# Two small products between TensorE's load of the verdict and its branch

## The chip, the cores and the metric

The kernel runs on one core of a Trainium2 chip. A core has TensorE (PE, the matmul array, with weight loads shown as PEld), VectorE (DVE), ScalarE (ACT), GpSimd (POOL) and SyncE (SP, which here issues the stores). Each engine has its own instruction stream, with a sequencer (shown with a q: DVEq, PEldq) that waits for semaphores, takes branches and hands instructions to the engine. Sixteen DMA engines serve all the queues. The metric is the device time of one execution in microseconds; the profile is of one more execution, whose time stands in the table below. Fp32 throughout.

## The reference

```python
# gated linear attention, B=4, H=8, S=768, D=48
state = alpha[:, :, t, :, None] * state + einsum('bhd,bhe->bhde', k[:, :, t], v[:, :, t])
y[:, :, t] = einsum('bhd,bhde->bhe', q[:, :, t], state)
# x: (B, H, S, D) -> (3072 tokens, 384)
h = x @ w_in          # 384 x 2048
g = h - tanh(h)
out = g @ w_out       # 2048 x 384
```

## The kernel before

The 3072 tokens are worked through in twelve units of 256. Of each unit the attention is computed first, and then its block with tanh in eight steps of 256 columns of the hidden layer: first products into h, h - tanh(h) as a polynomial on ScalarE and VectorE, second products into the output sums. From the seventh unit on the first products, and from the third on the second products, are made with fewer block products on combinations of blocks (Strassen's manner). So a unit's result does not lie in PSUM as such: it lies in four sums o0 to o3, which store() turns into two tiles. ScalarE scales o2 into p52, then VectorE makes four sums with put(), each 128 x 384: same = o1 + p52, cross = o1 - p52, same = same + o3, same = same + o0. Then SP issues four stores, two of cross and two of same.

The polynomial holds for small h alone, and the weights are rounded in a way that holds for a range alone. So the kernel gathers evidence while it works (tiles over, sizes, least, most, tiny). judge() (L1454 on) reduces it to one column, gather() (L1469) transposes that column with a matmul into one row of a PSUM tile of two banks (two_banks), VectorE reduces the row to one word ok (L1475), and see() (L1477) loads ok into a register of every engine. Behind fast() stands a branch (L1522): where ok is 0, every engine runs general(), a slow way that always holds; where it is 1, as here, every engine jumps over it to the closing semaphores. The code of general() lies between the branch and its target. On TensorE that is some 800 instructions.

The order of all work is written out. A planner lists tasks with an engine, a cost, a rank and what they come after, a long list of steps gives their order, and the instructions are emitted in that order, each into its engine's stream. The last tasks are the second products of the last step, see, and store of the last unit, which is emitted after see: so on each engine the load of the verdict stands ahead of what store() emits there, and behind store() comes the branch. TensorE has no instruction of store(): its last products of o3 and o0 come ahead of its load, and its branch follows the load at once. Semaphores are added by the framework wherever an instruction reads what another engine wrote or overwrites what another engine reads.

Lines that matter below: L1358 second products; L1418 p52 on ScalarE; L1421 the four sums in put() on VectorE; L1429 the stores; L1471 the transpose and L1475 the reduction of the verdict; L1478 its load; L1522 branch and what stands at its target; L1549 the closing barrier.

Of the kernel before, what the change touches and what calls it, by code (L numbers as in the profile page):

```python
# [17 lines left out]
HP = 64  # L18
# [415 lines left out]
def fast(tc, q, k, v, alpha, moe_w_in, moe_w_out, out, w_in, w_out, ident, ok, pad_rows):  # L434
# [7 lines left out]
    NU = B * UPB  # L442
# [7 lines left out]
    V, A, T, GP = nc.vector, nc.scalar, nc.tensor, nc.gpsimd  # L450
# [3 lines left out]
    with ExitStack() as ctx:  # L454
# [90 lines left out]
        def two_banks():  # L545
            return ps_sc.tile([P, 2, NP, P], FP32, name="sc")
# [30 lines left out]
        for n, (what, s) in enumerate(pieces):  # L577
            rank = RANK[what] + 2 * s
            held = pieces[n - 4] if n >= 4 else None
            both = what == "in" and s < BOTH_QUEUES  # L580
# [656 lines left out]
        def moe(u, rank, gait):  # L1237
# [170 lines left out]
            def store():  # L1408
                o = m["o"]
                if plain:  # L1410
                    for c in range(CU):
                        ob = two.tile([P, d_model], FP32, name=("same", "cross")[c], bufs=1)
                        A.mul(ob, o[c], 1 / W_SCALE)
                        nc.sync.dma_start(out=out_r[u * CU + c], in_=ob)
                    return

                p52, same, cross = (two.tile([P, 2, NH], FP32, name=n, bufs=1) for n in ("p52", "same", "cross"))
                A.mul(p52, o[2], 1 / W_SCALE)  # L1418

                def put(out, of, op, more):  # L1420
                    V.scalar_tensor_tensor(out=out, in0=of, scalar=1 / W_SCALE, in1=more, op0=ALU.mult, op1=op)  # L1421
                put(same, o[1], ALU.add, p52)
                put(cross, o[1][:, ::-1, :], ALU.subtract, p52)
                put(same, o[3], ALU.add, same)
                put(same, o[0][:, 0:1, :].to_broadcast([P, 2, NH]), ALU.add, same)
                for t, to in ((cross, 1), (same, 0)):
                    for c in range(CU):
                        n = abs(to - c)
                        nc.sync.dma_start(out=out_r[u * CU + c][:, n * NH:(n + 1) * NH], in_=t[:, c, :])  # L1429
            add(f"store {u}", "DVE", 2.1 if not plain else 0.1, rank + gait * FS + 4.9,  # L1430
                [f"second {u}:{FS - 1}", u == NU - 1 and "see"], store, lat=1.0)
            yield

# [18 lines left out]
        verdict = {}  # L1452
# [14 lines left out]
            verdict["fine"] = fine  # L1467

        def gather():  # L1469
            verdict["row"] = two_banks()[:, 0, 0, :]  # L1470
            T.transpose(verdict["row"][0:1, :], verdict["fine"][:, 0:1], ident)  # L1471
        add("judge", "DVE", 1.2, 16 * NU, [f"large {last_step}", f"x {NU - 1}.{CU - 1}", f"least {NU - 1}"] + [f"look {n}" for n in range(len(pieces))], judge)
        add("gather", "PE", 0.3, 16 * NU - 20, ["judge"], gather)
        add("ok", "DVE", 0.3, 16 * NU, ["gather"],
            lambda: V.tensor_reduce(out=ok, in_=verdict["row"][0:1, :], axis=AX.X, op=ALU.min))  # L1475
# [78 lines left out]
```

## Time and profile before

| | |
|---|---|
| median of 3 runs | 558.7 us (557.97, 558.70, 559.77) |
| profiled execution, its own time | 559.94 us |
| its span, first to last instruction | 558.12 us |
| busy: PE, DVE, ACT, POOL | 547.1, 462.2, 357.3, 4.9 us |
| granted TensorE clock | 0.999 |
| code loads: q8 (TensorE's), q14 (the others') | 49 of 16 KB, 24 of 8 KB |
| stores from L1429, issue to landing | 1.6 to 3.9 us, median 1.7 |

The page gives the busy time of each engine and its share of the span. Below the page the trace can be asked for a line, a stretch or a queue: times in such answers are from the start of the span, an arrow in brackets names what ended the idle time ahead of an instruction, and the number ahead of it is that idle time. Code loads are the DMA of instructions into an engine's instruction memory. The landing of a store is reported in 16 parts, one for each DMA engine. Where a time is given with three decimals or as a packet's start or end, it is read from the trace's records of instructions, DMA packets and semaphores.

### The profile page before, as it was taken

To read this page: it belongs to the slowest core of one execution; us is meant where nothing else is said; L and a number is where in the kernel's file an instruction comes from. 1 tells how busy PE (TensorE), PEld (TensorE's weight loads), DVE (VectorE), ACT (ScalarE), POOL (GpSimd) and SP (SyncE) were. 2 spreads that over 40 slices of the span, in tenths; PEclk is the share of its full clock that TensorE was granted. 3 is DMA by queue.
4 is the path that set the end of the run, shared out by engine and by line. 5 is a ranking of instruction groups with operands and counts; after the bars stand their busy time and mean duration, and the time that the engine had idled before them with its cause. 6 is when DMAs were issued, how large, how long until landed. Compare 5 with 4: busy or idle time off the path is not lost. (4 is left out here: it accounts for less than half of the span.)

```text
span 558.1 us, 14664 instructions
## 1 busy us (share of the span) xinstructions
PE 547.1 (98%) x6045; PEld 497.3 (89%) x6045; DVE 462.2 (83%) x853; ACT 357.3 (64%) x722; POOL 4.9 (1%) x23
## 2 busy tenths in 40 slices
PE   8999999999999999999999999999999999999995
PEld 7787777779998999999999999899999999999995
DVE  7988799999998597598896799999899856765764
ACT  3699995648666677667794556768556544545550
POOL 3000000000000000000000000000000000000000
PEclk9999999999999999999999999999999999999999
DMA  9999862144682483464540041311200000000001
GB/s 237 199 249 259 283 144 58 30 119 117 131 161 69 93 207 98 113 128 137 156 136 0 31 94 30 80 43 31 56 10 3 29 8 3 31 7 1 29 2 33
DMA packets 60233, 50.86 MB, mean 91 GB/s; under 512 B 35552, under 2 KB 49920, under 8 KB 60160
## 3 DMA queue, kind: packets, MB, share of 16 engines
q1 hardware_dynamic: 57536, 49.07, 35.1%
q8 instruction: 49, 0.80, 0.6%
q10 hardware_dynamic: 2624, 0.79, 0.6%
q14 instruction: 24, 0.20, 0.1%
HBM read 44.04 MB, written 4.72 MB: 87 GB/s over the span
## 5 line engine op out<-in xcount | busy, mean ns | idle before, releaser
L1256 PE MATMUL h<-xT,w_in 128*128 128x256 f32 (+1 forms) x588 | 131.2, 377 | 1.4 <-DVE w_in L92 0.7
L1256 PEld LDWEIGHTS h<-xT,w_in 128*128 128x128 f32 x588 | 108.7, 190 | 16.8 <-DVE w_in L92 1.1
L1358 PE MATMUL o<-b,e 128*128 128x192 f32 x480 | 93.3, 327 | 0.0
L1358 PEld LDWEIGHTS o<-b,e 128*128 128x128 f32 x480 | 78.9, 191 | 0.4
L1358 PE MATMUL o<-w_out,e 128*128 128x192 f32 x320 | 78.7, 328 | 0.4 <-issue 0.4
L1312 DVE SCALAR_TENSOR_TENSOR g<-z,w 128x512 f32<-128x512 f32 x96 | 64.7, 683 | 5.5 <-ACT z L1303 2.3
L1358 PE MATMUL o<-b,g 128*128 128x192 f32 x320 | 68.8, 326 | 0.0
L1303 ACT ACTIVATE z<-u 128x512 f32<-128x512 f32 x96 | 60.4, 632 | 3.7 <-DVE g L1312 2.1
L1293 DVE TENSOR_TENSOR w<-h,u 128x512 f32<-128x512 f32 x48 | 33.0, 686 | 34.5 <-PE h L1288 34.5
L1299 ACT ACTIVATE u<-w 128x512 f32<-128x512 f32 x48 | 30.0, 627 | 41.9 <-DVE w L1293 41.7
L1358 PEld LDWEIGHTS o<-w_out,e 128*128 128x128 f32 x320 | 55.1, 191 | 1.7 <-issue 0.5
L1267 PE MATMUL h<-xT,w_in 128*128 128x128 f32 x288 | 54.7, 278 | 0.2
L1280 ACT COPY u<-h 128x128 f32<-128x128 f32 x96 | 24.6, 265 | 47.1 <-PE h L1267 47.0
L1358 PEld LDWEIGHTS o<-b,g 128*128 128x128 f32 x320 | 53.8, 191 | 0.1
L1267 PE MATMUL h<-xT,w_out 128*128 128x128 f32 x288 | 53.3, 275 | 0.0
L1318 ACT ACTIVATE big<-u 128x1024 f32<-128x1024 f32 x48 | 50.7, 1056 | 0.6
L1267 PEld LDWEIGHTS h<-xT,w_in 128*128 128x128 f32 x288 | 48.2, 191 | 2.4 <-ACT xT L1038 0.4
L1288 PE MATMUL h<-xT,w_in 128*128 128x256 f32 x192 | 48.9, 380 | 0.0
L1299 ACT ACTIVATE u<-h 128x512 f32<-128x512 f32 x48 | 28.5, 594 | 29.5 <-PE h L1256 29.3
L1325 DVE TENSOR_TENSOR e<-g 128x384 f32<-128x384 f32 x80 | 44.1, 551 | 2.6 <-PE o L1358 0.8
L1308 DVE TENSOR_TENSOR w<-h,u 128x512 f32<-128x512 f32 x48 | 32.6, 682 | 15.5 <-ACT u L1299 15.5
L1267 PEld LDWEIGHTS h<-xT,w_out 128*128 128x128 f32 x288 | 44.1, 192 | 0.1
(171 smaller groups left out, 969.8 us busy)
## 6 DMA issues: line engine op xcount, KB each, us to landing
raw<-in_moe_w_out_dram SPq DMA_DIRECT2D x16, 768.0 KB, 6.1
raw<-in_moe_w_in_dram SPq DMA_DIRECT2D x48, 96.0 KB, 5.3
raw<-in_moe_w_in_dram SPq DMA_DIRECT2D x16, 288.0 KB, 5.3
vt<-in_v_dram SPq DMA_DIRECT2D x23, 192.0 KB, 3.7
ar<-in_alpha_dram SPq DMA_DIRECT2D x20, 192.0 KB, 3.3
kr<-in_k_dram SPq DMA_DIRECT2D x20, 192.0 KB, 3.2
qr<-in_q_dram SPq DMA_DIRECT2D x20, 192.0 KB, 3.2
raw<-in_moe_w_in_dram SPq DMA_DIRECT2D x16, 192.0 KB, 5.4
```

Source lines behind the costliest of these rows:

```text
L1256: T.matmul(h[:, a, to], lhsT=w_in[:, j, f * P:(f + 1) * P], rhs=xT[u][:, j, to], start=(j == 0), stop=(j == KT - 1))
L1267: T.matmul(m["h", s][:, to], lhsT=left[n][:, s], rhs=right[u][n], start=start, stop=True, skip_group_check=True)
L1280: A.copy(m["kept", s][:, n], m["h", s][:, 3])
L1288: T.matmul(m["h", s][:, 2 * a:2 * a + 2].rearrange("p i t -> p (i t)"), lhsT=wi[:, KT - 1, s, a], rhs=xT[u][:, KT - 1, :], start=False, st ...
L1293: V.tensor_add(m["w", s], m["h", s].rearrange("p i t -> p (i t)"), m["u", s])
L1299: A.activation(m["u", s], m["h", s], AF.Square, scale=W_SCALE ** -1.5)
L1303: A.activation(m["z", s], m["u", s], AF.Square, bias=QB, scale=QA * W_SCALE)
L1308: V.tensor_mul(m["w", s], m["h", s], m["u", s])
L1312: V.scalar_tensor_tensor(out=g.rearrange("p a c t -> p (a c t)"), in0=m["z", s], scalar=QK, in1=m["w", s], op0=ALU.add, op1=ALU.mult)
L1318: A.activation(big, m["us", s // 2].rearrange("p s t -> p (s t)"), AF.Relu, bias=-U_FAST, scale=W_SCALE, accum_out=over[:, n:n + 1])
L1325: V.tensor_sub(e[:, 0:3, :], x[:, 3:4].to_broadcast([P, 3, P]), x[:, 0:3])
L1358: T.matmul(o[n][:, i], lhsT=g_, rhs=w_, start=(s_ == 0 and (n, i) in ((0, 0), (1, 0), (2, 1), (3, 0))), stop=(s_ == FS - 1), skip_group_ch ...
```

## The change

When store() handles the last unit, two matmuls are emitted behind the first sum. Each multiplies the identity with the first 64 columns of same, and writes 64 columns of the second bank of the PSUM tile whose first bank held the verdict's row. Nobody reads them. For this gather() keeps the whole tile as verdict["both"]. In TensorE's stream they come behind the load of the verdict and ahead of the branch.

```diff
                 put(same, o[1], ALU.add, p52)
+                if u == NU - 1:
+                    for n in range(2):
+                        T.matmul(verdict["both"][:, 1, n, 0:HP], lhsT=ident, rhs=same[:, 0, 0:HP], start=True, stop=True)
                 put(cross, o[1][:, ::-1, :], ALU.subtract, p52)
                 put(same, o[3], ALU.add, same)
                 put(same, o[0][:, 0:1, :].to_broadcast([P, 2, NH]), ALU.add, same)
...
         def gather():
-            verdict["row"] = two_banks()[:, 0, 0, :]
+            verdict["both"] = two_banks()
+            verdict["row"] = verdict["both"][:, 0, 0, :]
             T.transpose(verdict["row"][0:1, :], verdict["fine"][:, 0:1], ident)
```

P is 128, HP is 64, NH is 192, NU is 12 and u is the unit. The orders of the other engines' instructions stay as they were.

## The prediction

> **What bounds the kernel now.** The page comes first.
>
> ```profile
> span 558.1 us, 14664 instructions
> PE 547.1 (98%) x6045; PEld 497.3 (89%) x6045; DVE 462.2 (83%) x853; ACT 357.3 (64%) x722; POOL 4.9 (1%) x23
> ```
>
> TensorE bounds the body, but nothing in the body is touched: the change lies in the last 9 us. So the second view is the timeline from 549 us (start, length, engine, line, operation).
>
> ```profile
> 549.54 2.11 PE L1358 MATMUL o<-b,e 128*128 128x192 f32 x12
> 549.74 0.49 ACT L1418 ACTIVATE p<-o 128x384 f32<-128x384 f32 x1 [5.11 <-PE o L1358]
> 550.26 0.56 DVE L1421 SCALAR_TENSOR_TENSOR same<-o,p 128x384 f32<-128x384 f32 x1 [1.55 <-ACTq L1522]
> 550.74 0.55 DVE L1421 SCALAR_TENSOR_TENSOR cross<-o,p 128x384 f32<-128x384 f32 x1
> 551.20 1.21 DVE L1421 SCALAR_TENSOR_TENSOR same<-o,same 128x384 f32<-128x384 f32 x2
> 551.31 0.81 SPq L1429 DMA_DIRECT2D out_dram<-cross  x2
> 552.44 0.82 SPq L1429 DMA_DIRECT2D out_dram<-same  x2
> ```
>
> Four sums, four stores; the last store is issued at 552.81 and yet the span lasts to 558.12. The third view is the line of the branch, which every engine runs after its load of the verdict (PEldq is TensorE's sequencer; shortest, median and longest in ns, first and last start).
>
> ```profile
> L1522 POOLq COMPARE_BRANCH  x1: 45/45/45, 549.3 to 549.3; - x1
> L1522 PEldq COMPARE_BRANCH  x1: 3762/3762/3762, 549.4 to 549.4; - x1
> L1522 ACTq COMPARE_BRANCH  x1: 50/50/50, 549.7 to 549.7; - x1
> L1522 DVEq COMPARE_BRANCH  x1: 72/72/72, 551.9 to 551.9; - x1
> L1522 PEldq EVENT_SEMAPHORE  x1: 51/51/51, 553.2 to 553.2; - x1
> L1522 SPq COMPARE_BRANCH  x1: 50/50/50, 553.3 to 553.3; - x1
> ```
>
> TensorE's branch takes 3.76 us. The DMA records say why: q8, which TensorE's code comes over, moves 16 KB from 550.40 for 1.38 us; TensorE goes on at 553.12 and 0.84 us later q8 moves another 16 KB. That one is in the fourth view, the DMA queues from 553.95 to 555.56 (packets, MB, share of 16 engines).
>
> ```profile
> q1 hardware_dynamic: 76, 0.05, 9.5%
> q8 instruction: 1, 0.02, 6.2%
> ```
>
> The fifth are the landings of the two last stores of `same`, and what SP waits for at the end (us in all, times, longest).
>
> ```profile
> DMA to landing us min/median/max: 2.2/3.0/3.8
> ```
>
> ```profile
> SPq L1522 <- SPq L1522: 3.0, 3, 2.0
> ```
>
> The last store lands 3.8 us after its issue, the one before it after 2.2. Of its 16 parts 15 have landed by 554.93, most by 554.52; the sixteenth at 556.61. Its eight packets start at 555.53, when the fetch (553.96 for 1.59 us) ends: one DMA engine served the code first. SP waits 2.0 us for it and then needs 1.5 us of closing semaphores. So the end is set by the last landing, and that by TensorE's second code fetch: 556.61 - 554.93 = 1.68 us.
>
> **The change, part by part.** It adds two fp32 products on TensorE, eight instructions (weight load and matmul, two passes each), in the stretch between its load and its branch; no other engine gets an instruction or another order, no DMA is added. But each product reads `same` and the third sum overwrites it. Two waits follow: TensorE's first added load waits for the first sum, with the branch alone behind it; VectorE's third sum waits for the second product, with the fourth sum, the two stores of `same` and VectorE's branch behind it.
>
> *The branch.* The first sum ends at 550.82. TensorE reaches the added load at about 549.36, where the branch stood, and waits 1.5 us. Does the sequencer wait, or only the array? On ScalarE the branch starts 6 ns after an ACTIVATE that had waited 5.11 us, on VectorE 24 ns after the fourth sum: the wait holds the sequencer. With 0.03 us to wake and eight issues (bounds 0.02 us each, a semaphore instruction of 17 to 21 ns, and 0.08, the array's own pace) the branch starts at 551.05 to 551.5; I take 551.1, since 30 instructions stood issued ahead in this very stretch. By the row's own offsets the first fetch runs 552.1 to 553.5, TensorE goes on at 554.9 and the second fetch runs 555.7 to 557.3.
>
> *The third sum.* The array is busy until the last product of o0, whose last pass starts at 551.33. The added passes queue behind: the first 0.16 us later (the pitch of 192 columns), three more at 0.11 us (two passes of 128 columns take 0.38 with 278 ns each, so 0.105 apart; 64 columns are no slower), 551.81, and 0.23 to 0.28 to the end: 552.04 to 552.09. VectorE followed TensorE by 0.02 at the verdict's reduction, so the third sum starts at 552.09 instead of 551.20: +0.89. Its 0.56 is unchanged, and the fourth follows 0.03 to 0.09 behind as now. The stores of `same` go out 0.82 to 0.89 later; I take 0.85: 553.29 and 553.66.
>
> *The last landing.* Undisturbed parts land 1.71 us after issue (554.52), disturbed by other engines' fetches 2.12 (554.93): 555.37 to 555.78, and I take 555.5, as the 8 KB fetch of 553.06 that held up the 554.93 part is by then over. Against 556.61 that is -1.1 us (-0.8 to -1.25). TensorE's first fetch now falls on the stores of `cross`, which have until 555 to land: nothing, unless it lasts 1 us longer. TensorE itself is through at 555.0; SP needs that at 556.2. If that cover goes, the closing barrier waits for TensorE instead.
>
> Sum for the profiled execution: span 558.12 - 1.1 = 557.0, and with the 1.82 us around it (559.94 - 558.12) 558.84.
>
> *Against the median.* The profiled execution lies 1.24 above the median of 558.7 and 0.17 above the highest run; the runs spread 1.80, close to the 1.68 that the late part costs. The race is near: that engine's eight packets were due from 553.77 and need 0.26 us, the fetch came at 553.96. I read the lowest run (557.97) as one that escaped. For it the change is a loss: 554.93 (or 554.52) becomes 555.5, +0.6 to +0.9, hence 558.6 to 558.8; the highest becomes 559.77 - 1.1 = 558.7. Both ends meet, so the changed kernel should show 558.6, hardly off the median, with less spread.
>
> *A rule against the rows.* The Trainium skill, "Runtime: NRT & Kernel Launch", section "Instruction fetch mechanics", says that a taken branch out of the two-page window stalls for the target page, and that crossing a 16 KiB boundary is mostly hidden. The stall agrees with 3.76 us here. By the second half the fetch at 553.96 would cost nothing and the change would be a pure loss of 0.85; the row prices that fetch at 1.68, and the row decides.
>
> **The rivals.**
>
> (A) Slower: the second fetch again meets the last store. The engine that carries q8 is free at 553.5 and must then pass 16 packets of `cross` and 16 of `same` before 555.7: 69 ns each. For: after the 16 KB fetch the eight packets took 85 to 98 ns. Against: after the 8 KB fetch of 552.80 they went at 33 ns at once. If it happens, the last part starts at 557.3, takes 0.6 and lands 0.46 later, 558.4: +1.8 on the profiled run, 560.4 to 561.6 in the timed ones.
>
> (B) Faster by over 0.3%: the third sum hardly waits and the collision goes. The last landing is then 554.5 to 554.9, -1.7 to -2.1: 556.6 to 557.0 from the median. Against it stands the array's queue, worked out above. With the delay, and if all three runs had been hit alike, it is 558.7 - 1.1 = 557.6, inside the bound.
>
> (C) The change doesn't move the branch, because the wait sits in the array's queue. The fetches stay, the stores come 0.85 later into the fetch of 553.96, and 16 packets instead of eight wait for 555.55: landing 556.9 to 557.3, +0.3 to +0.7, 559.0 to 559.4. The ScalarE row speaks against it.
>
> (D) TensorE ends last: if the closing code needs the second page, it waits for 557.3 and the 1.3 us that lay between fetch and resumption, 558.6, where the closing steps of 557.55 are now due at 556.4: +1.1, 559.8. Against: TensorE's closing rows are few.
>
> **How the numbers follow.** 0.3%, 1.68 us, is about what a measurement of this kernel can tell from no change. Forecast 0.56, C 0.09 and D 0.05 lie within it; A 0.18 is slower; B 0.10 is faster, and 0.01 is left to either side for what I don't see. So faster 0.11, same 0.70, slower 0.19. The time is the forecast's, 558.6. The range leaves out the worse half of A and nearly all of B: from 557.3 (all runs hit, largest gain 1.25, with 0.15 for the spread) to 560.5 (A's near end).
>
> **What would show it.** TensorE's branch at 551.1 and still some 3.8 us long; third sum at 552.1; stores of `same` at 553.3 and 553.7; the second 16 KB after 555.5; the last landing under 2.2 us from issue; span 557.0. Wrong if the branch stays at 549.4 (C), if the last landing is again over 3.5 us (A), or if the third sum starts before 551.8 (B).

## The result, and the profile after

The changed kernel takes 561.1 us, the median of six runs (560.5 to 562.92); the kernel before took 558.64 in the six runs beside it (557.97 to 559.77). The ratio is 1.0034 with a 95% interval of 1.002 to 1.0048: slower by 1.9 us (1.1 to 2.7); the two medians lie 2.5 us apart, inside that interval. The forecast was 558.6 with 560.5 as its upper end. The profiled execution took 560.74 us, its span is 559.0, and the 1.7 us around the span are close to the 1.8 of before.

The page first: the totals, which show that the body is as it was, with the four added matmuls in PE's count.

```profile
span 559.0 us, 14671 instructions
PE 547.3 (98%) x6049; PEld 497.5 (89%) x6049; DVE 462.5 (83%) x853; ACT 357.3 (64%) x722; POOL 4.9 (1%) x23
```

Then the timeline of the changed kernel at its end (start, length, engine, line, operation).

```profile
549.77 0.56 DVE L1421 SCALAR_TENSOR_TENSOR same<-o,p 128x384 f32<-128x384 f32 x1 [1.54 <-ACTq L1526]
550.24 0.55 DVE L1421 SCALAR_TENSOR_TENSOR cross<-o,p 128x384 f32<-128x384 f32 x1
550.82 2.53 SPq L1432 DMA_DIRECT2D out_dram<-cross  x2
550.84 0.58 PEld L1425 LDWEIGHTS sc<-same,ident 128*128 128x128 f32 x4
551.00 0.55 PE L1425 MATMUL sc<-same,ident 128*128 128x64 f32 x4
551.59 1.15 DVE L1421 SCALAR_TENSOR_TENSOR same<-o,same 128x384 f32<-128x384 f32 x2 [0.80 <-PE sc L1425]
553.45 0.97 SPq L1432 DMA_DIRECT2D out_dram<-same  x2
```

The products and the third sum behave as forecast: the sum waits 0.80 us for the second product. The surprise is in SP's row: the two stores of `cross` took 2.53 us to issue, where the kernel before needed 0.81. The rows of the stores, first that of `cross` before and then those of the changed kernel (shortest, median and longest in ns, first and last start; below them issue to landing) show that it was the second of the pair, with 2156 ns instead of 431.

```profile
L1429 SPq DMA_DIRECT2D out_dram<-cross x2: 332/382/431, 551.3 to 551.7; - x2
```

```profile
L1432 SPq DMA_DIRECT2D out_dram<-cross x2: 332/1244/2156, 550.8 to 551.2; - x2
L1432 SPq DMA_DIRECT2D out_dram<-same x2: 430/462/494, 553.5 to 554.0; - x2
...
DMA to landing us min/median/max: 1.8/3.3/3.6
```

The rows of the branch, and of the closing barrier, of the changed kernel (PEldq is TensorE's sequencer; a DRAIN is the instruction with which an engine reports to the closing barrier), and last TensorE's DRAIN in the kernel before:

```profile
L1526 PEldq COMPARE_BRANCH  x1: 3898/3898/3898, 550.4 to 550.4; - x1
...
L1526 DVEq COMPARE_BRANCH  x1: 72/72/72, 552.2 to 552.2; - x1
L1526 PEldq EVENT_SEMAPHORE  x1: 51/51/51, 554.3 to 554.3; - x1
```

```profile
L1553 SPq DRAIN  x3: 7/7/7, 558.2 to 558.5; - x3
...
L1553 PEldq DRAIN  x2: 8/8/8, 557.7 to 558.6; - x2
```

```profile
L1549 PEldq DRAIN  x2: 8/8/8, 553.3 to 557.7; - x2
```

TensorE's first DRAIN stands at 557.7, 3.4 us behind its first closing semaphore at 554.3; before, it stood at 553.3, 0.15 behind the semaphore. It is late now, but SP's, which waits for the last store, is later still: 558.2. SP's longest wait there is 2.2 us:

```profile
SPq L1526 <- SPq L1526: 2.7, 2, 2.2
```

The body up to the tail differs from execution to execution (the first of the four sums starts anywhere from 549.2 to 550.5 us in the fourteen traces of this case), so from here on all times of the tail are counted from the start of the first sum, and "tail" is what lies from there to the end of the span. They are read from the records of instructions, DMA packets and landings. "First load" and "second load" are the two 16 KB code loads of q8.

| us behind the first sum's start | before | after | difference |
|---|---|---|---|
| TensorE's branch | -0.906 | 0.617 | +1.52 |
| first load, start and end | 0.138, 1.517 | 1.636, 3.211 | +1.50, +1.69 |
| third and fourth sum start | 0.939, 1.590 | 1.818, 2.410 | +0.88, +0.82 |
| length of the issue of the second `cross` store | 0.431 | 2.156 | +1.73 |
| `same` stores issued | 2.175, 2.551 | 3.684, 4.223 | +1.51, +1.67 |
| second load, start and end | 3.695, 5.286 | 5.380, 6.659 | +1.69, +1.37 |
| last landing | 6.344 | 7.733 | +1.39 |
| TensorE's first closing DRAIN | 3.064 | 7.938 | +4.87 |
| tail | 7.860 | 9.249 | +1.39 |

The loss is in the last landing, to the hundredth, and that follows the end of the second load in both kernels, 1.06 us and 1.07 us behind it. Of the changed kernel's last store fifteen of sixteen parts had landed by 5.92; the sixteenth came at 7.73, after that load.

### The profile page after: what moved, and what is told of

It reads as the page before. It is cut to its first block, busy times and chain, and to the rows that moved or that the text cites. A ratio compares the mean times of both kernels' runs of the same rounds, so it can differ in the third digit from the quotient of the medians.

```text
span 559.0 us, 14671 instructions
## 1 busy us (share of the span) xinstructions
PE 547.3 (98%) x6049; PEld 497.5 (89%) x6049; DVE 462.5 (83%) x853; ACT 357.3 (64%) x722; POOL 4.9 (1%) x23
## 4 chain that ended last, share of the span: by engine, by line
PE 93%; DVE 3%; ACT 2%; issue 1%; POOL 0%; DVEq 0%; ACTq 0%; POOLq 0%
PE o L1358 32%; PE h L1256 22%; PE h L1267 13%; PE o L1336 7%; PE h L1288 7%; PE h L989 4%; PE sc L962 1%; PE sc L1135 1%; DVE same L1421 1%; PE sc L969 1%; PE sc L989 1%; PE turned L731 1%; DVE w L1293 1%; ACT u L1299 1%; PE spin L1443 0%
```

## The experiments

Three explanations stand against each other, told here by name. **The issue stall**: SP's second `cross` store is held up by the first load, which now runs while it is issued; the `same` stores go out late and meet the second load again. **The sums' delay**: the third sum's 0.88 us alone make the difference. **The late DRAIN**: the eight added TensorE instructions shift the closing code within its pages (the 16 KB pieces that a load brings), so that TensorE's DRAIN waits for the second load. In the recorded expectations theory 1 is the forecast's own account (the waits and a race), the late DRAIN is theory 3, and the sums' delay is theory 2 (in the first of them that number means something else). The stall has no place in the first four; it first stands as the rival in the last of the second four, and then as theory 6. The medians of the kernel before were 559.29, 559.65 and 559.18 us beside the first, second and third four kernels; a kernel is compared only with the median beside it.

### The first four: what each part does alone

*The kernel before once more*, no edit.

> The kernel before, unchanged, to see its spans run by run. Theory 1 (a race between TensorE's second code load and the last store): the time is about 558.6, and the profile shows one of two pictures: the last store landing 3.8 us after its issue with a time near 559.9, or within 2.2 us with a time near 558. Theory 2 (the late landing belongs to every execution, the spread of the runs comes from the body): the last store lands 3.5 us or more after issue also in an execution of 558.6 or less.

It took 559.48 us, ratio 1.0006 (0.9984 to 1.0028). The row of issue to landing of its stores, and below it that of the next kernel, have the late part again:

```profile
DMA to landing us min/median/max: 1.6/2.0/3.8
```

```profile
DMA to landing us min/median/max: 1.6/2.0/3.9
```

The collision with the second load is in each of the three profiled executions that have stores and code loads at the times of before. That speaks for a regular collision, and not for a race that some executions escape; that some of the timed executions, which have no trace, escape it isn't excluded.

*The products without their read of `same`*: same instructions in the same places, but no wait in either direction.

```diff
-T.matmul(verdict["both"][:, 1, n, 0:HP], lhsT=ident, rhs=same[:, 0, 0:HP], start=True, stop=True)
+T.matmul(verdict["both"][:, 1, n, 0:HP], lhsT=ident, rhs=ident[:, 0:HP], start=True, stop=True)
```

> The two products stay where the change puts them, but read the identity instead of the first sum: TensorE waits for nothing, VectorE waits for nothing, eight instructions more in TensorE's code. Theory 1 (the waits do it): branch of TensorE at 0.9 us ahead of the first sum as before, third sum undelayed, time as before, 558.3 to 559.0. Theory 3 (the code moved by eight instructions so that TensorE's closing DRAIN lies in the next code page): the DRAIN comes 1.3 us behind the end of the second 16 KB load instead of 0.15 us behind the branch, and the time is 0.5 to 1.5 above before, 559.1 to 560.1.

It took 558.99 us, ratio 1.0 (0.9977 to 1.0022); its tail is 7.927. Branch, loads, sums and stores stand where they stood before. One thing has moved, in these rows of the branch and of the closing barrier:

```profile
L1526 PEldq EVENT_SEMAPHORE  x1: 51/51/51, 552.2 to 552.2; - x1
```

```profile
L1553 PEldq DRAIN  x2: 8/8/8, 555.9 to 556.7; - x2
```

The first DRAIN comes 3.7 us behind the semaphore instead of 0.15, and 1.37 behind the end of the second load. So the late DRAIN is the work of the eight instructions, not of the read. Here it is hidden: SP is ready 0.43 later (7.131 against 6.704). Eight more instructions on TensorE, with no wait, cost nothing that the interval (some 1.2 us to either side) can tell.

*VectorE's wait without TensorE's*: on the kernel before, two sums that nobody reads, behind the `cross` sum.

```diff
                 put(cross, o[1][:, ::-1, :], ALU.subtract, p52)
+                if u == NU - 1:
+                    idle = two.tile([P, N * (P + 1)], FP32, name="idle", tag="junk", bufs=1)[:, 0:d_model]
+                    for n in range(2):
+                        V.tensor_add(idle, same.rearrange("p a n -> p (a n)"), p52.rearrange("p a n -> p (a n)"))
```

> The kernel before with two idle sums of 128x384 on VectorE ahead of the third sum, which holds it up by about 0.93 us as the change does (0.88), while TensorE's code and its branch stay. Theory 1: the second code load (4.6 us behind the unmoved branch) now catches both stores of the last tile in every execution; last landing 0.3 to 0.7 later than in the disturbed execution of before, time 560.0 to 560.6. Theory 2 (VectorE's wait is all the cost, at its length): 558.64 + 0.93 = 559.6. Theory 4 (the moved branch is what costs): 559.2 to 559.6, and clearly under the 561.1 of the change.

It took 559.48 us, ratio 0.9999 (0.9977 to 1.0021), although the third sum came 1.24 us late, more than the 0.88 of the change. The 1.4 to 2.0 us of theory 1 lie outside that interval; the 0.9 of theory 2 does not, so the times alone don't exclude it. In the trace it isn't there: the tail is 7.714, below 7.860. The second load ran at 3.315 to 4.566, before most of the late stores, and the last landing at 6.198 no longer followed it: all sixteen parts of the last store landed from 6.02 on. What made them late is in this row:

```profile
L1433 SPq DMA_DIRECT2D out_dram<-same x2: 332/727/1122, 553.3 to 553.6; - x2
```

A store issued in the time of a code load is held up here too: the second store of `same` took 1.122 us, and was through 0.363 us after the second load's end. The delayed sums thus traded one loss for another of about its size.

*The change with two filler products left out at the start of the program*, so that TensorE's closing code lies at the same offset as before (`spin` emits products that only fill TensorE's time; nobody uses their results).

```diff
+        left_out = []
+
         def spin(by=ident):
+            left_out.append(by)
+            if len(left_out) in (10, 11):
+                return
...
```

> The change with two filler products (eight instructions) of TensorE's start left out, so that all code from there on lies in its pages as before. Theory 3: TensorE's closing DRAIN comes within 0.2 us of the branch's end, and if the DRAIN of 557.7 had a part in the end, the time falls by 0.5 or more, to 560.6 or less. Theory 1: the DRAIN moves, the time doesn't: 560.7 to 561.3, since the last landing stands at 557.5 in either case.

It took 558.66 us, ratio 0.9993 (0.9973 to 1.0014), not to be told from before. TensorE's DRAIN came at once (4.204, behind a branch that ended at 3.996). But in the profiled execution a second thing was gone, which this edit doesn't touch:

```profile
L1432 SPq DMA_DIRECT2D out_dram<-cross x2: 332/382/431, 550.8 to 551.1; - x2
L1432 SPq DMA_DIRECT2D out_dram<-same x2: 332/382/431, 552.7 to 553.1; - x2
...
DMA to landing us min/median/max: 1.9/2.3/2.7
```

No store was held up. The first load started where it does in the changed kernel (1.636) and was short, 0.966 us instead of 1.575. The `same` stores went out at 2.995 and 3.371 (+0.82 to before, the sums' delay), the last landing was at 5.239, the tail 6.756: 1.10 us below before. Two explanations now shared the loss, and one kernel that misses both didn't tell them apart.

### The second four: which of the two

*The change once more*, no edit.

> The change, unchanged, beside the next three on one chip. Theory 3 (the eight instructions put TensorE's closing DRAIN on the next code page, and the closing barrier then waits for that page): 1.0 to 2.5 us over before, and the DRAIN at the end of the second 16 KB load + 1.3 us, 7.3 to 8.0 us behind the start of the first sum. Theory 5 (it was that chip or that hour): as the realigned kernel, about before.

560.74 us, ratio 1.0021 (1.0004 to 1.0038), 1.1 us over the median beside it. Issue of the second `cross` store 2.315 us, last landing 8.144 (1.08 behind the second load), DRAIN 8.514 (7.3 to 8.0 had been expected), tail 9.660. Both are there again.

*The realigned change once more*, the same kernel as above.

> The change with two filler products of TensorE's start left out, a second time. Theory 3: 1.5 to 2.5 us below the change itself, 0.3 to 1.1 below before; DRAIN within 0.2 us of the branch's end, last landing 5.2 to 5.6 behind the start of the first sum. Theory 5: equal to the change within 0.5.

560.94 us, ratio 1.0026 (0.9997 to 1.0055), where 1.5 to 2.5 us below the change had been expected of the late DRAIN. Two of its eleven runs lay at 558.4 to 558.7, the others at 560.2 or more, where eight of twelve had been at 558.07 to 558.80 the first time. The rows of the profiled execution, its stores and then its closing barrier:

```profile
L1432 SPq DMA_DIRECT2D out_dram<-cross x2: 332/1274/2217, 550.9 to 551.3; - x2
...
DMA to landing us min/median/max: 1.8/3.5/3.8
```

```profile
L1558 PEldq DRAIN  x2: 8/8/8, 554.8 to 559.1; - x2
```

The DRAIN comes at 554.8, at once, and the tail is still 9.633. The late DRAIN falls as the cause of the loss in this execution: the stall is enough by itself. The first load lasted 1.634 us here; the second ended at 7.060, and nine packets of the last store started only from 7.045 on, where all others had started by 5.62. The landing was at 8.117. The same program thus either stalls or doesn't.

*One product instead of two.*

```diff
-                    for n in range(2):
+                    for n in range(1):
```

> The change with one product instead of two: four instructions instead of eight, no filler left out. The closing EVENT_SEMAPHORE of the changed kernel (two instructions ahead of the DRAIN) still came at once, so the page ends at most two instructions behind it; with four instructions less the DRAIN lies ahead of the end. Theory 3: DRAIN at once again, third sum 0.22 earlier than in the change, time as the realigned kernel or 0.2 better. Theory 1 (the wait and the race alone): as the change, less 0.2.

560.5 us, ratio 1.0019 (0.9998 to 1.0041), tail 9.264. The third sum came at 1.595 instead of 1.818, the issue still took 2.038 us, and ended 0.370 after the first load:

```profile
L1432 SPq DMA_DIRECT2D out_dram<-cross x2: 332/1185/2038, 551.0 to 551.4; - x2
```

```profile
L1553 PEldq DRAIN  x2: 8/8/8, 558.1 to 558.8; - x2
```

The time decides nothing: with 560.94, 560.74 and 560.5 us the realigned change, the change and this kernel lie too close in these four to tell either theory from the other. In the trace the stall sets the stores' time, not the sums. The DRAIN was a miss: it was expected at once with four added instructions and is late (8.147, 1.47 behind the second load). Where the closing code crosses into the second page was counted wrongly; why four suffice stays open.

*The products read `cross` instead of `same`*, behind the `cross` sum, realigned as above: the third sum is free of the wait, the branch waits 0.46 us longer still.

```diff
                 put(cross, o[1][:, ::-1, :], ALU.subtract, p52)
+                if u == NU - 1:
+                    for n in range(2):
+                        T.matmul(verdict["both"][:, 1, n, 0:HP], lhsT=ident, rhs=cross[:, 0, 0:HP], start=True, stop=True)
                 put(same, o[3], ALU.add, same)
```

> The realigned kernel with the products reading cross, which nobody overwrites: VectorE's third sum has no TensorE product to wait for (-0.88), the branch comes 0.47 later than in the change (1.1 behind the start of the first sum). Theory 1: first code load at 2.1 to 3.5, stores of same issued at 2.2 and 2.6 as before, second code load from 5.5, behind the last landing of 4.4 to 4.9; end 0.4 to 0.9 below the realigned kernel. Rival: the first code load now holds up one DMA engine while SP issues, the issue of the next store stalls by 0.7 to 1.7 as in the change, and nothing is gained on the realigned kernel.

559.12 us, ratio 1.0 (0.9978 to 1.0022), 0.5 below the median beside it without being told from it. Branch at 1.080, first load from 2.138 to 3.858. The `cross` stores were out by then, and the stall moved to the next pair that is issued in the time of the load:

```profile
L1432 SPq DMA_DIRECT2D out_dram<-same x2: 332/977/1622, 552.1 to 552.4; - x2
```

It ended 0.316 after the load. The last store landed at 5.687, ahead of the second load (6.026), and the tail is 7.203. The stall is what the expectation's rival forecast, and the landing misses the 4.4 to 4.9 of its theory 1. So a stall costs little where what it delays still passes ahead of the second load.

### The third four: the stores on two queues

If an issue is held up because two stores stand in one queue behind a load, the second store of each pair on ScalarE's idle queue should not be. The edit, alone and on three of the kernels above:

```diff
-nc.sync.dma_start(out=out_r[u * CU + c][:, n * NH:(n + 1) * NH], in_=t[:, c, :])
+(nc.scalar if u == NU - 1 and c else nc.sync).dma_start(out=out_r[u * CU + c][:, n * NH:(n + 1) * NH], in_=t[:, c, :])
```

*On the kernel before.*

> The kernel before, with the second of the two stores of cross and of the two of same of the last unit issued by ScalarE, which is idle by then. Nothing else is changed. Theory 6 (the end is the last landing, late by TensorE's second code load; a queue has one store outstanding on the engine that loads code, a second one stalls): both stores of same are issued 2.18 behind the start of the first sum, their packets are through by 3.5, ahead of the second load at 3.7; last landing 4.1 to 4.6 instead of 6.3 to 6.4, tail from the first sum 5.8 to 6.4 instead of 7.9, time 1.5 to 2.1 below before. Rival: ScalarE's own branch and code load move to 3.6 and catch the stores, landing 5 or later, gain under 1.

558.19 us, ratio 0.9985 (0.9973 to 0.9996): the lowest median of all, 1.0 us below that of the kernel before beside it. That is less than the 1.5 to 2.1 us expected. The timeline and the landings:

```profile
550.85 0.33 SPq L1429 DMA_DIRECT2D out_dram<-cross  x1
550.86 0.37 ACTq L1429 DMA_DIRECT2D out_dram<-cross  x1
551.98 0.33 SPq L1429 DMA_DIRECT2D out_dram<-same  x1
551.98 0.37 ACTq L1429 DMA_DIRECT2D out_dram<-same  x1
```

```profile
DMA to landing us min/median/max: 1.7/2.1/2.5
```

The last store goes out 0.37 earlier than before, and none of its packets waits for the end of the second load (3.677 to 4.841): all had started by 4.003. Last landing 4.639 instead of 6.344, tail 6.229 instead of 7.860. The collision that the kernel before pays in its trace is worth these 1.63 us of tail; the 0.6 us between that and the medians' difference were not traced.

*On the change, realigned.*

> The change with the two filler products left out and the stores on two queues. The sums stay 0.82 late and the branch stays moved. Theory 6: no issue waits for the first code load any more (0.3 to 0.5 instead of 2.0 to 2.3 us), both stores of same go out at 3.0, land by 5.3, ahead of the second load at 5.4; tail 6.6 to 6.9 instead of 9.2 to 9.7. Theory 2 (the sums' delay is the cost): issue times don't matter, the tail stays 8.5 or more.

558.77 us, ratio 0.9988 (0.9979 to 0.9997). No stall (issues of 0.33 and 0.37 us, the last pair at 2.996), the DRAIN at 4.920, last landing 5.568, tail 7.159. The sums' delay is there in full and the kernel isn't slower than before, so this delay alone doesn't make the change slower. It isn't free either, now that the collision is gone: against *two_queues* the tail is 0.93 longer and the median 0.6 higher, though the intervals don't separate the two. The tail is a little above the 6.6 to 6.9 expected; now the load came late: it started at 2.165, 1.55 after the branch, where it otherwise took 1.0.

*On the change as it is.*

> The same without the fillers left out: TensorE's closing DRAIN comes late again, 1.3 to 1.5 us behind the end of the second code load. If that DRAIN can set the end where the stores don't, the tail is 8.5 to 9.2, about 2 us over the realigned one; if the closing barrier doesn't depend on it, 6.6 to 6.9 as there.

560.62 us, ratio 1.0027 (1.001 to 1.0043). Here no store is late (last landing 5.462), and it is as slow as the change. The rows of the closing barrier and SP's wait:

```profile
L1553 SPq DRAIN  x3: 7/7/7, 556.5 to 558.0; - x3
...
L1553 PEldq DRAIN  x2: 8/8/8, 557.7 to 558.0; - x2
```

```profile
SPq L1553 <- PEq L1553: 1.8, 2, 1.3
```

SP is ready at 556.5 and waits 1.3 us for TensorE, whose DRAIN comes at 557.7, 1.284 behind the second load; the tail is 8.219, under the 8.5 to 9.2 expected. Against the realigned kernel with the same queues the tail is 1.06 longer and the median 1.85, and no run of the one is as fast as the slowest of the other (559.93 and more against 559.37 and less): the late DRAIN, once nothing covers it, is enough by itself too. (The two filler products that the realigned kernel lacks lie far ahead of the tail; what they add to the median was not measured.)

*On the realigned kernel that reads `cross`.*

> Products reading cross (no delay of VectorE, branch at 1.08), fillers left out, stores on two queues. Theory 6: stores of same issued at 2.18 in both queues, the code engine's packets behind the first load (2.1 to 3.9), landing 4.6 to 5.0, tail 6.2 to 6.7; so moving the branch gains nothing on two_queues, and costs up to 0.5 through TensorE's own closing at 5.2 to 5.4.

559.21 us, ratio 0.9996 (0.9985 to 1.0007), tail 7.867 where 6.2 to 6.7 was expected. The stores went out as early as in the fastest kernel (2.177), but the first load started 1.82 after the branch, at 2.899, in the time of their packets; the branch took 4.678 us and the second load started only at 6.500. The tail is set by the last landing, 6.277: of each of the four stores one part landed last, at 5.7 to 6.3, and the 36 packets that were still missing at the end of the first load (4.317) started only from 4.312 on. So no issue stalls, but code and packets still delay each other.

## Why the prediction was wrong

**What held.** The end is set by the last landing, and that by the second code load. The wait holds TensorE's sequencer, so the branch moves; it is still 3.9 us long; the offsets from the branch to the first load (1.02 us, before 1.04) held. The third sum came +0.88 (forecast +0.89) and the fourth +0.82. The rival that the branch doesn't move is out, and so is the one in which the third sum hardly waits.

**The branch**, a small miss. It started 59 ns after the first sum's end, at 0.617: in the times of the profile before this is 550.88, 0.17 ahead of the lower bound of 551.05 (its own terms add up to 551.01, and the trace has 25 instructions that started behind the branch, not 30). The eight instructions took less than the row of a semaphore instruction suggested.

**The last landing, the step that failed.** It was put as: "TensorE's first fetch now falls on the stores of `cross`, which have until 555 to land: nothing, unless it lasts 1 us longer." The landings of `cross` were indeed not what counted. Their issue was. The step priced the load against packets under way and not against the queue's next issue: SP stood 2.156 us in the second `cross` store and could not issue `same`, whose sums were done 0.6 us before the end of that issue. So the `same` stores went out +1.51 and +1.67 instead of +0.85, and were again in the queue when the second load came. The end of a held-up issue lies behind the end of a load by much the same time in all six traces that have one of over 1 us:

| trace | held-up store | length of its issue, us | its end behind the load's end, us |
|---|---|---|---|
| after | second of `cross` | 2.156 | 0.370 |
| after, once more | second of `cross` | 2.315 | 0.371 |
| realigned, once more | second of `cross` | 2.217 | 0.384 |
| one product | second of `cross` | 2.038 | 0.370 |
| sums delayed alone | second of `same` | 1.122 | 0.363 |
| reads `cross`, realigned | second of `same` | 1.622 | 0.316 |

Two milder cases fit: in the kernel before once more and in the one without the read, the issue of the second `cross` store took 0.481 us instead of 0.431 and ended 0.378 and 0.371 behind the first load. A load under way doesn't always hold an issue up, though: in the first trace of the realigned kernel the issue went on from 1.425 to 1.856 while the load ran from 1.636 on. The 8 KB loads of the other engines don't seem to make the difference: one ran at 2.446 to 2.882 in that trace and at 2.258 to 2.807 in the one that stalled for 2.156 us.

With that, rival A came true, at its price: it gave 560.4 to 561.6 and the measured median is 561.1. Its mechanism was half right. It has the second load meet the last store because the engine behind q8 is slow to pass the packets; the runs show that the stores were issued late, so that its price fits is in part luck. (Of the eight packets that it has at 85 to 98 ns, seven took 78 to 107 and the last 36; their 0.6 us in all stands.) The forecast of -1.1 us was not wrong as arithmetic: in the one traced execution with its stores on one queue in which no issue stalled and the DRAIN came at once, the tail was 1.10 below before.

**"TensorE itself is through at 555.0", and rival D.** This was wrong too, and the last landing hid it. D was put at 0.05 because "TensorE's closing rows are few". Their number doesn't matter, their place does: with four or eight more instructions ahead, the first DRAIN came 1.28 to 1.47 us behind the second load in each of five traces, as rival D had it (1.3). With the stores out of the way, the change loses by this alone. The change thus has two sufficient causes of a loss, and its own profile shows the larger one only.

**Against the median.** The spread of the runs was read as a race that some executions escape, which made the gain and the loss meet at 558.6. All three traces with stores and loads at their old times show the collision, and the body alone, up to the first sum, differs by 1.3 us among the fourteen. The spread is no evidence of a race. The loss of 0.6 to 0.9 that this step gave an undisturbed execution (by its own figures 0.6 to 1.0, as 555.5 less 554.52 is 0.98) fits the two kernels on two queues, with and without the delayed sums: 0.93 of tail, 0.6 in the medians, the latter not clear of the noise. What has no support is that the fastest executions of the kernel before were undisturbed ones.

**The rule.** The prediction let the row decide against the Trainium skill, "Runtime: NRT & Kernel Launch", section "Instruction fetch mechanics", by which crossing into the next page is mostly hidden. That choice holds: in seven traces the last landing lies 1.05 to 1.08 us behind the end of the second load, and in five the DRAIN waits for it.

**What stays open.** Why the first trace of the realigned kernel didn't stall, though the load began at the same place: its load was short (0.966 us), but what decides between the two cases wasn't found, nor why the share of runs at 558 changed from eight of twelve to two of eleven. Why four instructions make the DRAIN late. And why, in the second trace of the realigned kernel, nine packets waited from 5.62 on for a load that is recorded from 6.10. How a load holds up an issue, and why on one queue alone, is argued from the times here, not shown.

## What to carry to other kernels

A taken branch over far code makes transfers of its own, here 1.0 us behind the branch and again 0.7 to 1.4 us after the engine goes on: before moving a branch, or work ahead of it, look at which DMA issues and landings lie in these two stretches, and count the issuing engine's next instruction among what a load can hold up. Where the last stores of a kernel stand in one queue, a second idle queue is cheap to try; it gave the only clear gain here, 1.0 us in the medians. And a few instructions added ahead of closing code can make that code wait for a code load (four and eight did here), so an engine that is "done early" has to be looked at again after every change of its stream.

## What the runs showed of the hardware

A code load can hold up the issue of a store, not only its packets: 0.43 us became 1.1 to 2.3 us, ending 0.32 to 0.38 us after the load. With the stores on two queues the first load came late by 0.5 and 0.8 us in two traces (1.55 and 1.82 us behind the branch instead of 1.0), and with it TensorE's branch took up to 4.678 us; in the third with a moved branch, the change as it is, branch and stores stood as in the first of these and the load came after 1.0, so that the packets delay it is likely but not shown. A load of 16 KB takes 0.96 to 1.75 us in the tails above, and 0.97 and 1.63 us for the first load of one and the same program. And the sequencer hands over its eight instructions and takes the branch within 59 ns of the sum that it waited for.
